# Storing the split gate weights in DRAM for a second pass of a state-space and gated-product kernel

## The chip, the cores and the metric

The kernel runs on one core of a Trainium2 chip. The core has a matrix engine (TensorE, PE in the profile; PEld is its weight load), a vector engine (VectorE, DVE), a scalar engine (ScalarE, ACT), GpSimd (POOL) and a sync engine (SyncE, SP) that only issues transfers; transfers run on 16 DMA engines. Each engine works through its own instructions in order and waits for others through semaphores. The metric is the device time of one execution in microseconds. A profile is one execution recorded by the hardware profiler.

## The reference

Everything is in fp32, for one sequence of 2048 tokens of width 640.

```python
mod = (_silu(c) @ w_mod).reshape(c.shape[0], 6, 1, -1)
sa, ca, ga, sb, cb, gb = (mod[:, 0], mod[:, 1], mod[:, 2], mod[:, 3], mod[:, 4], mod[:, 5])
h = _layernorm(x, axis=-1) * (1 + ca) + sa
x = x + ga * _A_ref(h, ...)          # a long convolution: kernel K from 192 complex modes a channel, by FFT
h = _layernorm(x, axis=-1) * (1 + cb) + sb
x = x + gb * _B_ref(h, ...)
...
def _B_ref(x, w_gate, w_up, w_down):     # w_gate, w_up: 640 x 1536, w_down: 1536 x 640
    g = jnp.einsum("bsd,df->bsf", x, w_gate)
    u = jnp.einsum("bsd,df->bsf", x, w_up)
    h = g * u
    return jnp.einsum("bsf,fd->bsd", h, w_down)
```

## The kernel before

There are two parts. The first, up to about 520 us, computes the modulation, the convolution kernel and the convolution. Its work is placed by a table of due times (`SCHED`): each unit (`u_d` is the last step of the convolution, `u_head` the start of the gated product) is advanced at written positions, and `SCHED["w"]` places the first loads and splits of gate weights among them. `u_d` loads two quarters of a transformed block (`TVa`, `TVb`, from `WD`) and the residual (`xsa`, `xsb`, from `A_u`) on the sync queue, multiplies on TensorE (L967), and adds the residual on DVE (L971 where the result stays in SBUF, L974 where it is stored). A row of matmuls without a use of its result (`warm`, L1149) runs in one gap.

The second part is the gated product. The 2048 tokens are worked in two halves (`for half in range(2)`), each of two token blocks of 512 columns. In a half, a loop over the 12 blocks `f` of 128 hidden columns computes gate and up products for both token blocks at once with a scheme that replaces eight products by seven with sums of weights and of tokens. After it come the down projections of the half's two token blocks (`down`, L1463), 12 steps each of 24 matmuls, and `fin`, which adds the residual and stores the output (L1475 and L1478).

TensorE multiplies in a reduced-precision form of fp32 (type `F32R`), and each product is made of three: high x high, high x low and low x high parts. So every weight and every activation is split by `hilo`: ACT copies it to the `F32R` type (the high part), DVE subtracts that from the value (the low part):

```python
def hilo(hi, lo, v):
    act(hi, v)
    V.tensor_tensor(lo, v, hi, op=OP.subtract)
```

The gate weights that the products `x_1` and `x_2` use come as pairs of blocks (`raw`, tile `wga`, 640 KB) and are split one block at a time by `split_g(i)` into `wsgh` and `wsgl`, four buffers each; the same buffers take the split down weights (`d_prep`). Block indices run to 24: block 12 + f of the second half has the same weights as block f of the first. `used` starts the next pair load after every second block. `raw_u` loads a gate block (`wgb`) and an up block (`wur`) again for the sums of weights; `sums_u` makes the sums on POOL (tile `tf`, L1036 to L1039) and `split_u` splits them (`wth`, `wtl`, `wsuh`, `wsul`). In a step of the loop `y_1`, `z_1`, `x_1`, `y_2`, `x_2`, `y_3`, `z_2` are groups of products, each in one of six PSUM banks; `y_2` has a sum on POOL (L1412), `y_3` a product on POOL (L1430). `split_g` is called four blocks ahead, between `y_2` and `sums_u`; the splits of blocks 12 to 14 are called in the last steps of the first half's last down projection, that of block 15 at the beginning of the second half. In the first half, `fold` also scales the down weights and stores them in DRAM (`wdg`).

The order of instructions on each engine and queue is that of the program from the second part on (a scheduler is off); in the first part it follows from the due times.

Of the kernel before, what the change touches and what calls it, by code (L numbers as in the profile page):

```python
# [10 lines left out]
F32 = mybir.dt.float32  # L11
# [7 lines left out]
P = 128  # L19
# [4 lines left out]
NB = D // P  # L24
NF = F // P
# [77 lines left out]
    k=(  # L103
        (189, 202),
        (208, 226),
        (356, 358),
        (499, 559),
        (422, 496),
        (634, 660),
        (663, 672),  # L110
        (698, 713),
# [37 lines left out]
    h=(2480, 2716, 2875, 2876, 2878, 2878, 2878, 2878),  # L149
    g=(  # L150
# [5 lines left out]
    ),  # L156
# [68 lines left out]
def tile_kernel(ctx: ExitStack, tc: tile.TileContext, I, out):  # L225
    nc = tc.nc
    V, S, G, PE, SY = nc.vector, nc.scalar, nc.gpsimd, nc.tensor, nc.sync

    def act(o, i, f=AF.Copy, **kw):
        return S.activation(o, i, f, **kw)  # L230
# [3 lines left out]
    dram1 = ctx.enter_context(tc.tile_pool(name="dram1", bufs=1, space=DRAM))  # L234
# [35 lines left out]
    def need(n, *k):  # L270

        assert done.get(k, 0) >= n, k
# [468 lines left out]
    def kg_pool(n, part):  # L741
        hf, s = divmod(n, 4)
        if part == 0:
            mk_ph(n)
            return
        mk_eq(n)
        mk_ep(n)
# [50 lines left out]
    def kg_ma(n):  # L798
        if n % 2 == 0:
            kg_of[n // 2] = ps_kg.tile([P, 8, 64], F32, name="kg")  # L800
        kg = kg_of[n // 2]
        PtA, QtA = OUT[n]["PA"], OUT[n]["QA"]
        for dl in range(4):
            dd = (n % 2) * 4 + dl
            for c in range(2):
                for j in range(4):
                    PE.matmul(kg[j * 32 : j * 32 + 32, dd, :], PtA[:, c, dl * 4 + j, :], QtA[:, c, dl * 4 + j, :],  # L807
                              start=dd == 0 and c == 0, stop=False, tile_position=(0, j * 32))
        if n % 2:
            need(0 if n < 8 else 4, "dsk")  # L810
            PE.matmul(kg[:, :, 0], ident, dskt[:, n - 1 : n + 1, :].rearrange("p t l -> p (t l)"), start=False, stop=False)

    def kg_mb(n):
        kg = kg_of[n // 2]
        PtB, QtB = OUT[n]["PB"], OUT[n]["QB"]
        for dl in range(4):
            dd = (n % 2) * 4 + dl
            for c in range(2):
                for j in range(4):
                    lo = (j % 2) * 64  # L820
                    r = dl * 2 + j // 2
                    PE.matmul(kg[j * 32 : j * 32 + 32, dd, :], PtB[lo : lo + 64, c, r, :], QtB[lo : lo + 64, c, r, :],  # L822
                              start=False, stop=dd == 7 and c == 1, tile_position=(lo, j * 32))

    def kg_out(n):

        Kt = ring(fp, [P, 8, 64], "Kt")
        act(Kt.rearrange("p d (b q) -> p d b q", q=4), kg_of[n // 2].rearrange("p d (q b) -> p d b q", q=4))
        KT[n // 2] = Kt
# [148 lines left out]
    WS, WU, WT, WR, UX, UE, AT = {}, {}, {}, {}, {}, {}, {}  # L978

    def mk(n, shape, dt_=F32, bufs=1):  # L980

        if n in FIRST:
            return FIRST.pop(n)
        return (wp if n in LEFT else gp).tile(shape, dt_, name=n, bufs=bufs)
# [4 lines left out]

    PAIRS = []  # L990
    for h in range(2):
        PAIRS += [("g", h * NF + 2 * p) for p in range(NF // 2)]
        PAIRS += [("d", 2 * h + T, 2 * p) for T in range(2) for p in range(NF // 2)]

    def raw():
# [15 lines left out]
    def used(f):  # L1011
        if f % 2 and PAIRS:
            raw()
# [11 lines left out]

    def split_g(i):
        WS[i] = mk("wsgh", [P, NB, P], F32R, 4), mk("wsgl", [P, NB, P], F32R, 4)
        hilo(*WS[i], WR.pop(("g", i)))
        if i > 3:
            used(i)  # L1030

# [175 lines left out]
    def at(ts, g, *a):  # L1207

        it = g(*a)
        for v in ts:  # L1210
            jobs.setdefault(v // 10, []).append((v, it))

    def once(f):
        def g(*a):
            f(*a)
            return
            yield
        return g
# [17 lines left out]
    def due(x):  # L1236
        for _, g in sorted(jobs.pop(x, []), key=lambda j: j[0]):
            next(g, None)
# [63 lines left out]
    for t in range(3 * NK + 24):  # L1302
        n, g = divmod(t, 3)
        k = n < NK
        if k:
            (kg_aq, kg_ap, kg_b)[g](n)
        due(2 * t)
        if k:
            for f in MUL.pop(0):
                f()  # L1310
        due(2 * t + 1)
        if g < 2 and n + 1 < NK:
            kg_pool(n + 1, g)
        if g == 0 and 0 < n <= NK:
            kg_mb(n - 1)
        if g == 1 and n % 2 == 0 and 0 < n <= NK:
            kg_out(n - 1)
        if g == 2 and k:
            kg_ma(n)
        if t == 3 * NK + 1:  # L1320
            kgp.close()
            PF.append(fft.enter_context(tc.tile_pool(name="ps_t", bufs=3, space=PSUM)))
            ps_g = ctx.enter_context(tc.tile_pool(name="ps_g", bufs=2, space=PSUM, side="right"))
            wp = ctx.enter_context(tc.tile_pool(name="wp", bufs=1, reuse_waits="tile"))
            wdg = dram1.tile([P, NF, D], F32, name="wdg")
            wv = [I[n].rearrange("(k p) f -> p k f", p=P) for n in ("B_w_gate", "B_w_up", "B_w_down")]

            def rows(tb):
                need(NB - 2, "d", tb)
                SY.dma_start(XB[tb][:, :, 0 : (NB - 2) * P], x2d[:, 4 * tb : 4 * tb + 4, 0 : (NB - 2) * P])  # L1330

            for j in range(2):
                XB[j] = mk(f"xb{j}", [P, 4, D])
                at(T0["wl"][j : j + 1], once(rows), j)
                at(T0["w"][j : j + 1], once(raw))
            for j in range(4):
                at(T0["w"][2 + j : 3 + j], once(split_g), j)
            at(T0["h"], u_head)
            at(T0["wm"][0:1], once(warm), 30)
            at(T0["wm"][1:2], once(warm), 4)  # L1340
# [191 lines left out]
    for half in range(2):  # L1532
# [37 lines left out]
        else:  # L1570
            for j in range(AHEAD):
                if LEAD <= j + 1 < AHEAD:
                    split_g(i0 + j + 1)
                x_1(i0 + j)
                x_2(i0 + j)
# [13 lines left out]
        for f in range(NF):  # L1589
            i = i0 + f  # L1590
            y_1(i)
            z_1(i)
            late = 0 < f <= NF - AHEAD
            if late:
                x_1(i + AHEAD - 1)
            if f + 1 < NF:
                split_u(i + 1, "a")
            y_2(i)
            if f + 1 < NF:
                split_u(i + 1, "bc")  # L1600
            if f + AHEAD < NF:
                split_g(i + AHEAD)
            if f + 2 < NF:
                sums_u(i + 2)
            if f + 3 < NF:
                raw_u(i + 3)
            if late:
                x_2(i + AHEAD - 1)
            y_3(i)
            z_2(i)  # L1610
            if half == 0:
                fold(f)
            if f >= NF - 2:
                d_prep(2 * half, f - NF + 2)
# [37 lines left out]
```

## Time and profile before

| | |
|---|---|
| time, median of 3 runs | 1004.66 us (1000.55 to 1005.87) |
| the profiled execution | 1001.29 us, span 999.2 us |
| busy: PE, DVE, ACT, POOL | 900.0, 762.8, 561.9, 564.3 us |
| moved by DMA | 153.16 MB, 153 GB/s on average |
| mean granted TensorE clock | 0.961 |

The span runs from the first to the last instruction; the execution's own time has 2.1 us more. Rows of groups give line, engine, operation, output <- inputs, shape and count, then busy time and mean ns. Rows of the timeline give start and length in us, engine, line, operation and, in brackets, the idle time before it with what ended it. SPq rows are issues on the sync queue, not the transfers themselves. Rows of DMA issues give count, KB of one and the median us from issue to landing. A chain row gives start, length and what the last-ending chain of work was doing.

### The profile page before, as it was taken

How to read it: one execution, taken by the hardware profiler on the slowest of the kernel's cores; microseconds unless marked ns; L12 is line 12 of the kernel's file. 1: busy time of each engine (PE TensorE's matmuls, PEld its weight loads, DVE VectorE, ACT ScalarE, POOL GpSimd, SP SyncE). 2: the span in 40 equal slices, each digit the busy share in tenths (PEclk: the TensorE clock that was granted, in tenths of full speed). 3: DMA queues.
4: the chain of work that ended last, by engine and by line, in shares of the span. 5: the costliest groups of instructions: out<-in, count | busy, mean ns of one | idle time of the engine just before them, and what ended most of it. 6: DMA issues, size and time to landing. Idle time of an engine off the chain costs nothing.

```text
span 999.2 us, 26832 instructions
## 1 busy us (share of the span) xinstructions
PE 900.0 (90%) x11192; PEld 727.2 (73%) x11192; DVE 762.8 (76%) x1399; ACT 561.9 (56%) x1048; POOL 564.3 (56%) x415
## 2 busy tenths in 40 slices
PE   4867898899789689998888999999999999999998
PEld 3565556675576467776555888879998888889998
DVE  8798569889979997975769788777576887768452
ACT  4869989987878979752354323235463422223331
POOL 5978899799789899930032667650112365542000
PEclk9877889999899899999999999999999999999999
DMA  8728754555256454577673442535635232212341
GB/s 265 254 50 301 227 176 135 194 163 167 68 163 202 129 161 120 164 248 214 210 210 123 153 150 87 184 132 159 209 134 202 88 105 80 79 53 59 100 159 53
DMA packets 147817, 153.16 MB, mean 153 GB/s; under 512 B 9200, under 2 KB 125424, under 8 KB 146288
## 3 DMA queue, kind: packets, MB, share of 16 engines
q1 hardware_dynamic: 145968, 148.43, 46.8%
q10 hardware_dynamic: 1728, 3.02, 0.8%
q8 instruction: 88, 1.44, 0.6%
q14 instruction: 33, 0.27, 0.1%
HBM read 110.45 MB, written 40.96 MB: 152 GB/s over the span
## 4 chain that ended last, share of the span: by engine, by line
PE 63%; DVE 16%; ACT 10%; issue 4%; DMA 4%; POOL 2%; SPq 1%; DVEq 0%; ACTq 0%; POOLq 0%
PE pa L1059 26%; PE pa L1463 16%; PE kg L807 2%; DMA xsb<-A_u 2%; PE kg L822 2%; PE psfc L889 2%; ACT L230 1%; PE psfb L889 1%; PE psfa L889 1%; PE psfc L946 1%; PE psfb L946 1%; PE psfa L946 1%; PE psfc L868 1%; ACT trb L230 1%; PE psfa L844 1%
## 5 line engine op out<-in xcount | busy, mean ns | idle before, releaser
L710 POOL TENSOR_TENSOR EQ<-LQ,RH 128x1536 f32<-128x1536 f32 x40 | 124.2, 3105 | 9.9 <-DVE QtB L767 9.7
L230 ACT ACTIVATE z<-pa 128x512 f32<-128x512 f32 x24 | 14.4, 598 | 175.7 <-POOL a L1430 112.1
L1024 DVE TENSOR_TENSOR wsgl<-wga,wsgh 128x640 fp32r<-128x640 f32 x72 | 70.0, 976 | 46.1 <-ACT wsgh L230 46.1
L1412 POOL TENSOR_TENSOR z<-z,s 128x512 f32<-128x512 f32 x24 | 32.1, 1337 | 126.5 <-DVE s L1411 72.0
L230 ACT ACTIVATE wsgh<-wga 128x640 fp32r<-128x640 f32 x72 | 52.5, 732 | 65.1 <-PE pa L1463 47.9
L1024 DVE TENSOR_TENSOR wtl<-tf,wth 128x256 fp32r<-128x256 f32 (+1 forms) x72 | 42.7, 594 | 48.3 <-ACT wth L230 48.3
L1463 PE MATMUL pa<-wsgh,sh 128*128 128x384 f32 (+1 forms) x304 | 69.4, 309 | 0.0
L1463 PE MATMUL pa<-wsgh,sl 128*128 128x384 f32 (+1 forms) x304 | 69.0, 308 | 0.0
L1463 PE MATMUL pa<-wsgl,sh 128*128 128x384 f32 (+1 forms) x304 | 69.0, 308 | 0.0
L710 POOL TENSOR_TENSOR Phb<-LH,DH 128x1536 int32<-128x1536 int32 x20 | 62.3, 3115 | 11.2 <-ACT tra L230 11.2
L710 POOL TENSOR_TENSOR EP<-LP,RH 128x768 f32<-128x768 f32 x40 | 66.1, 1651 | 0.0
L710 POOL TENSOR_TENSOR Pha<-LH,DH 128x1536 int32<-128x1536 int32 (+1 forms) x21 | 62.5, 2974 | 2.2 <-ACT trb L230 1.9
L1036 POOL TENSOR_TENSOR tf<-wur,wgb 128x256 f32<-128x256 f32 x23 | 17.8, 776 | 75.6 <-DVE wtl L1024 50.0
L822 PE MATMUL kg<-QtB,PtB 64*32 64x64 f32 x2560 | 48.7, 229 | 5.4 <-DVE QtB L766 5.3
L822 PEld LDWEIGHTS kg<-QtB,PtB 64*32 64x32 f32 x2560 | 41.6, 114 | 15.4 <-issue 6.5
L1463 PEld LDWEIGHTS pa<-wsgh,sl 128*128 128x128 f32 x304 | 46.4, 187 | 0.0
L1463 PEld LDWEIGHTS pa<-wsgl,sh 128*128 128x128 f32 x304 | 46.3, 187 | 0.0
L1059 PE MATMUL pa<-sh,wtl 128*128 128x512 f32 x144 | 45.0, 394 | 1.4 <-DVE wtl L1024 1.2
L1463 PEld LDWEIGHTS pa<-wsgh,sh 128*128 128x128 f32 x304 | 46.3, 187 | 0.0
L1059 PE MATMUL pa<-sh,wth 128*128 128x512 f32 x144 | 44.9, 393 | 0.5 <-ACT wth L230 0.5
L1059 PE MATMUL pa<-sl,wth 128*128 128x512 f32 x144 | 44.5, 390 | 0.0
L1430 POOL TENSOR_TENSOR a<-s,z 128x512 f32<-128x512 f32 x24 | 38.8, 1618 | 5.4 <-DVE s L1429 5.4
(604 smaller groups left out, 2925.2 us busy)
## 6 DMA issues: line engine op xcount, KB each, us to landing
wga<-wdg SPq DMA_DIRECT2D x24, 640.0 KB, 5.0
wga<-B_w_gate SPq DMA_DIRECT2D x12, 640.0 KB, 5.9
wgb<-B_w_gate SPq DMA_DIRECT2D x24, 320.0 KB, 3.4
wur<-B_w_up SPq DMA_DIRECT2D x24, 320.0 KB, 4.0
xb<-x2d SPq DMA_DIRECT2D x6, 1280.0 KB, 5.7
TVb<-WD SPq DMA_DIRECT2D x22, 256.0 KB, 3.6
t_tw<-w_mod SPq DMA_DIRECT2D x3, 1600.0 KB, 8.5
t_ti<-w_mod SPq DMA_DIRECT2D x3, 1600.0 KB, 7.9
```

Source lines behind the costliest of these rows:

```text
L230: return S.activation(o, i, f, **kw)
L710: G.tensor_tensor(o.rearrange("p x (h l) -> p x h l", l=8), lo.unsqueeze(2).to_broadcast([P, rows, nh, 8]), hi.rearrange("p h x -> p x h") ...
L807: PE.matmul(kg[j * 32 : j * 32 + 32, dd, :], PtA[:, c, dl * 4 + j, :], QtA[:, c, dl * 4 + j, :], start=dd == 0 and c == 0, stop=False, til ...
L822: PE.matmul(kg[j * 32 : j * 32 + 32, dd, :], PtB[lo : lo + 64, c, r, :], QtB[lo : lo + 64, c, r, :], start=False, stop=dd == 7 and c == 1, ...
L889: PE.matmul(r[c][par * 64 : par * 64 + 64, i, :], t_tw[:, k0 + k, c, :], src[:, k, :], start=True, stop=True, tile_position=(0, par * 64))
L946: PE.matmul(r[par][:, i], t_ti[lo : lo + 64, qd * 4 + i, c, :], x[lo : lo + 64, c, i, :], start=c == 0, stop=c == 1, tile_position=(lo, 0))
L1024: V.tensor_tensor(lo, v, hi, op=OP.subtract)
L1036: E.tensor_tensor(t[:, 0:2], u[:, 0:2], g[:, 0:2], op=OP.subtract)
L1059: PE.matmul(ps, w[a][:, k], x[b][:, l], start=n == 0 and m == 0, stop=n == 2 and m == len(ks) - 1)
L1412: G.tensor_tensor(ZT[i], ZT[i], S67[i], op=OP.add)
L1430: G.tensor_tensor(a_tile(NF + i % NF), c, ZT.pop(i), op=OP.mult)
L1463: PE.matmul(ACC[tb][t][c], x[:, ts], w[:, cs], start=st, stop=f == NF - 1 and n == 2 and (c == 0 or t % 2 == 1))
```

## The change

When the first half makes the high and the low part of a gate block, both are also stored to a DRAM tensor `wsd`, on the sync queue, 320 KB each. The second half no longer loads pairs of gate blocks for `x_1` and `x_2` and does not split them: for blocks 12 to 23 `split_g` issues two loads from `wsd` into `wsgh` and `wsgl` on GpSimd's queue. The DRAM tensor has the type fp32 and the tiles the type `F32R`, so the loads are casting transfers.

```diff
     PAIRS = []
     for h in range(2):
-        PAIRS += [("g", h * NF + 2 * p) for p in range(NF // 2)]
+        PAIRS += [("g", 2 * p) for p in range(NF // 2)] if h == 0 else []
         PAIRS += [("d", 2 * h + T, 2 * p) for T in range(2) for p in range(NF // 2)]
...
     def split_g(i):
         WS[i] = mk("wsgh", [P, NB, P], F32R, 4), mk("wsgl", [P, NB, P], F32R, 4)
+        if i >= NF:
+            for j in range(2):
+                G.dma_start(WS[i][j].rearrange("p k m -> p (k m)"), wsd[:, i - NF, j])
+            return
         hilo(*WS[i], WR.pop(("g", i)))
+        for j in range(2):
+            SY.dma_start(wsd[:, i, j], WS[i][j].rearrange("p k m -> p (k m)").bitcast(F32))
         if i > 3:
             used(i)
...
             wdg = dram1.tile([P, NF, D], F32, name="wdg")
+            wsd = dram1.tile([P, NF, 2, NB * P], F32, name="wsd")
```

## The prediction

> **What bounds the kernel now.** I read the busy time by stretch first, to see which stages have room at all, then the chain of work that ended last.
>
> ```profile
> 765.00:910.00 145.00, 145.00 (x634) 118.47 (x633) 106.18 (x157) 45.48 (x101) 66.83 (x63) 1.00 0.30 94
> 752.00:765.00 13.00, 11.45 (x71) 10.51 (x70) 10.73 (x16) 5.55 (x9) 5.57 (x4) 1.00 0.23 87
> 910.00:999.00 89.00, 84.98 (x578) 84.57 (x576) 41.61 (x65) 27.03 (x44) 1.64 (x2) 1.00 0.33 104
> ```
>
> The columns of the stretches are: stretch, length, busy us of PE, PEld, DVE, ACT, POOL, granted clock, share of the DMA engines, GB/s. In the second half's loop (765 to 910) PE is busy for all 145.00 us of 145.00, while DVE has 39 us and ACT 100 us idle. Only 1.55 us of PE time are missing in the turn between the halves (752 to 765). The chain that ended last says the same, and shows where PE is not the bound:
>
> ```profile
> 485.24 7.95 PE psg L1149 x34
> 494.97 3.20 DMA xsb<-A_u
> 498.98 4.86 DMA xsb<-A_u
> 503.96 0.69 DVE xsb L974
> 544.52 103.91 PE pa L1059 x451
> 761.34 149.04 PE pa L1059 x648
> 910.38 84.62 PE pa L1463 x576
> ```
>
> From 544.52 for 103.91 us and from 761.34 for 149.04 us the chain is one unbroken row of matmuls. Between 485 and 504, at the end of the convolution, it runs through loads of the sync queue. So the change works at three places: it relieves engines in the second half, where PE sets the time; it puts loads on GpSimd's queue there; and it puts stores into the sync queue where that queue sets the time.
>
> **What is removed.** Twelve high parts on ACT, twelve low parts on DVE, and six loads of a pair of gate blocks.
>
> ```profile
> L1024 DVE TENSOR_TENSOR wsgl<-wga,wsgh 128x640 fp32r<-128x640 f32 x72 | 70.0, 976 | 46.1 <-ACT wsgh L230 46.1
> L230 ACT ACTIVATE wsgh<-wga 128x640 fp32r<-128x640 f32 x72 | 52.5, 732 | 65.1 <-PE pa L1463 47.9
> 758.89 1.92 DVE L1024 TENSOR_TENSOR wsgl<-wga,wsgh 128x640 fp32r<-128x640 f32 x1
> 759.34 0.45 PE L1463 MATMUL pa<-wsgl,hh 128*128 128x384 f32 x2
> 760.74 0.55 DVE L1475 TENSOR_TENSOR xb<-pa,xb 128x384 f32<-128x384 f32 x1
> 761.34 0.73 PE L1059 MATMUL pa<-hh,wsgh 128*128 128x512 f32 x2 [1.55 <-DVE xb L1475]
> ```
>
> 12 x 0.976 = 11.7 us leave DVE and 12 x 0.732 = 8.8 us leave ACT, nearly all beside a PE that is full, so they buy nothing there. One of the twelve is on the path: the split of block 14 holds DVE from 758.89 to 760.8, the first sum of the finishing step (L1475) comes behind it, and the first matmul of the second half waits 1.55 us for that sum to free its PSUM bank. Without the split the sum can run while the last matmuls still do: **-1.5 us** (at least 1.0, because the sum still has to follow the matmuls of its own bank; at most 1.55, the whole gap). What is late next is then the matmul row itself.
>
> **What is added in the second half: 24 loads on GpSimd's queue.** In the loop the two loads of block i+4 stand behind POOL's sum L1412 of step i and ahead of the four sums of block i+2 and the product L1430. The products of the first stage (x_1) of step i+1 need them. One step, as it is now:
>
> ```profile
> 829.69 1.34 POOL L1412 TENSOR_TENSOR z<-z,s 128x512 f32<-128x512 f32 x1 [4.66 <-ACT wsgh L230]
> 842.09 1.34 POOL L1412 TENSOR_TENSOR z<-z,s 128x512 f32<-128x512 f32 x1 [4.81 <-ACT wsgh L230]
> 844.53 0.74 POOL L1036 TENSOR_TENSOR tf<-wur,wgb 128x256 f32<-128x256 f32 x1 [1.10 <-DVE wtl L1024]
> 845.47 0.51 SPq L1020 DMA_DIRECT2D wur<-B_w_up  x1
> 847.92 1.76 POOL L1430 TENSOR_TENSOR a<-s,z 128x512 f32<-128x512 f32 x1
> 849.89 0.62 PE L1059 MATMUL pa<-hh,wsgh 128*128 128x512 f32 x2
> 850.35 0.63 PE L1059 MATMUL pa<-hh,wsgl 128*128 128x512 f32 x2
> 850.15 0.60 ACT L230 ACTIVATE z<-pa 128x512 f32<-128x512 f32 x1 [8.10 <-PE pa L1059]
> wur<-B_w_up SPq DMA_DIRECT2D x24, 320.0 KB, 4.0
> wga<-B_w_gate SPq DMA_DIRECT2D x12, 640.0 KB, 5.9
> out<-xb SPq DMA_DIRECT2D x12, 320.0 KB, 3.1
> ```
>
> A step takes 842.09 - 829.69 = 12.40 us. POOL is free at 843.43; the matmul that reads the low part starts at 850.35 (the high part is read at 849.89). So issuing both loads and landing the second may take 850.35 - 843.43 = 6.9 us. Call T the time that POOL spends on one issue and L the time from issue to landing: the load is in time if 2T + L is at most 6.9. The trace shows no load issued by POOL and no casting one, so both are bounded. T: at least the 0.51 us of a sync-queue issue, at most the 1.76 us of POOL's longest operation here; I take 1.1, the middle. L: at least 3.1 us (a 320 KB transfer with rows of 2560 B), at most 5.9 us (the 640 KB gate load, as if the cast halved the rate). I take 4.5: the up-weight load of the same size takes 4.0 us, and that load and its neighbour start at about 845, at the same time as these two. 2 x 1.1 + 4.5 = 6.7 us: just in time. Between the ends, 4.1 and 9.4 us, the stall per step is 0 to 2.5 us. A stall repeats, because POOL's L1412 of the next step moves with PE: eight steps issue loads for a later step, so 0 to 20 us. I take 0.25 us x 8 = **+2 us**.
>
> The Trainium skill, page "DMA: Bandwidth & Descriptors", section "Anatomy of one DMA — SWDGE (gpsimd) path", gives 2.0 us + bytes/436e3 for such a transfer, 2.75 us for these 327,680 B. By it the two loads would be in time with room, and the sum would be 2 us lower; no row here shows a transfer from POOL.
>
> What is queued behind the loads on POOL: the sums L1036 to L1039 and L1430. They have waited 1.10 us at 844.53 for DVE, so 2T = 2.2 us makes them 1.1 us later. L1430 ends at 850.8 instead of 849.68; ACT's copy, which needs it and begins at 850.15 because of PE, slips by about 0.7 us, on an engine that idled 8.10 us before it. No PE time. A hit between DVE and POOL hides in the 39 us that DVE idles. At the turn, the loads for blocks 12 to 15 each wait on POOL for a down-projection step to free their buffer, and queued behind them are the sums of the second half's tokens, read later. Three pieces of PE work lie between that release and x_1: down steps of 24 matmuls (84.62/576 x 24 = 3.5 us) or blocks of 15 (12.40/54 x 15 = 3.4 us), so 10.4 us against 6.7. Cost zero, up to 3 us if POOL's first issues are much slower than the rest.
>
> **What is added in the first half: 24 stores of 320 KB on the sync queue.** Those of blocks 4 to 11 lie ahead of weight loads, here in one step:
>
> ```profile
> 592.37 0.37 SPq L1018 DMA_DIRECT2D wgb<-B_w_gate  x1
> 593.92 0.51 SPq L1002 DMA_DIRECT2D wga<-B_w_gate  x1
> 600.11 0.73 ACT L230 ACTIVATE wsgh<-wga 128x640 fp32r<-128x640 f32 x1
> ```
>
> A store of a low part waits for DVE's split, so wgb and wur go out some 2 us later; they are read a step of 12.40 us on, with about 4 us to land. The pair load wga now runs a step ahead of its splits; behind the stores it goes out at about 594 of the step before its use, lands 5.9 us later plus 2 us for the stores' data, at 602, and ACT's split of 600.11 slips by 2 us. ACT has 8 us of idle time behind it, and DVE and x_1 take the parts later still. Zero for PE, which is unbroken for 103.91 us; if that cover were gone, 2 us in every second step, 8 in all.
>
> The eight stores of blocks 0 to 3 are another matter. The changed program has four of them between the loads TVb/xsa and TVa/xsb, and four more between TVa/xsb and TVb/xsb:
>
> ```profile
> 488.07 0.91 SPq L959 DMA_DIRECT2D TVa<-WD  x2
> 489.64 0.99 SPq L959 DMA_DIRECT2D TVb<-WD  x2
> 494.97 0.37 SPq L961 DMA_DIRECT2D xsb<-A_u  x1
> 488.10 3.01 DVE L1024 TENSOR_TENSOR wsgl<-wga,wsgh 128x640 fp32r<-128x640 f32 x4
> 494.25 0.69 DVE L971 TENSOR_TENSOR xb<-psfc,xsb 128x512 f32<-128x512 f32 x1 [2.53 <-PE psfc L967]
> 498.26 0.69 DVE L971 TENSOR_TENSOR xb<-psfa,xsb 128x512 f32<-128x512 f32 x1
> 488.00:490.00 2.00, 2.00 (x10) 1.65 (x10) 2.00 (x4) 0.35 (x1) 0.00 (x0) 1.00 0.23 69
> 490.00:492.00 2.00, 2.00 (x11) 1.65 (x10) 1.72 (x3) 0.00 (x0) 0.00 (x0) 1.00 1.11 315
> 494.00:496.00 2.00, 1.79 (x12) 0.31 (x8) 1.71 (x7) 0.00 (x0) 0.00 (x0) 1.00 0.01 2
> TVb<-WD SPq DMA_DIRECT2D x22, 256.0 KB, 3.6
> ```
>
> The first store goes early. The second waits for the first of DVE's four splits, 488.10 + 3.01/4 = 488.9; the third and fourth follow at about 0.5 us each, the fourth behind the second split. So TVa is issued at 490.4, not 488.07, and TVb, behind four more stores, at about 494, not 489.64. Their data count too. Three stores (0.98 MB), TVa (0.52) and xsb (0.26) make 1.77 MB; the engines, at 315 GB/s when full and with some 1.5 us from issue to full flow, need until 488.9 + 1.5 + 5.6 = 496. L971 then comes at about 497 instead of 494.25. Four more stores (1.31 MB) and TVb (0.52) take 5.8 us more, to 501.8, and with the matmuls of 1 to 1.5 us the second L971 stands at about 503 instead of 498.26: +5. The next xsb load waits for it as it does now and takes its 4.86 us, and L974, which heads the in-order DVE queue at 503.96, moves along. Everything up to 544 follows from that queue. **+5 us**. The lower end: if the stores' data did not delay the loads, TVa 2.3 us and TVb 4.4 us later on the queue would eat slack (matmuls of L1149 fill PE until 493.19; all data are in by 494.00, 4.3 us ahead of the second L971) and cost +1. The upper end, with the stores at half that rate, is +8. A gain is excluded: the order of the queue is fixed.
>
> **Sum.** -1.5 + 2 + 5 = +5.5 us. The profiled execution took 1001.29 us (span 999.2 and 2.1 around it); that makes 1006.8 there. The median of the runs shown is 3.4 us above that execution, so the forecast against the median 1004.66 is 1010.2.
>
> **Rivals.** *The casting loads land late* (POOL issues slowly, or the cast halves the rate): 2T + L of 9.4 us, 2.5 us in each of eight steps: +20 - 1.5 + 5 = +23.5, 1028. Decided where 2T + L passes 6.9 us; for it speak POOL's long operations (1.76 us) and a DVE that is busy 106 of 145 us and may get in POOL's way; against it, the 3.1 us store row. The Trainium skill, page "SBUF — State Buffer", section "SBUF: two separate sides", warns that DVE in a two-port mode keeps GpSimd from writing descriptors, which would put the loads into this rival; the same page's section "Who interferes with whom" exempts the two-input subtraction, which is most of what DVE runs here, and no run yet shows it.
>
> *The stores are absorbed*, so that it is not slower: the transfers of the tail drain fast enough that the second L971 comes by 499.3. Then the end of the convolution costs +1, the loads are in time, and the turn gains 1.5: -0.5, 1004.2. Decided by whether TVb lands before 498; for it speak engines idle at 494 to 496 (2 GB/s), against it that 2.6 MB of stores need 8.3 us at 315 GB/s in a window that has 2 us free.
>
> *Relief counts for more* than the one gap: impossible from the rows by more than a little, as PE has 1.55 us idle in the turn, none in the loop, and 4.02 us at the very end, where the output leaves: at most -5.
>
> **How the numbers follow.** Forecast case (+2 to +9) 0.52, late loads (+9 to +25) 0.25, absorbed (-3 to +2) 0.17, relief or something not seen 0.06. 0.5% is 5.0 us, about what a measurement can tell from no change. Of the forecast case two thirds lie above that (its upper ends are farther off than its lower ones): 0.35 + 0.25 = 0.60 slower. Faster by 0.5% gets the last case's 0.06. The rest, 0.34, is no change. The range leaves out the end of the late loads and the last case: 1003 to 1028.
>
> **What would show it.** Right: the stores' issues at 489 to 494 ahead of TVb, the second L971 at about 503, the first matmul at the turn without a gap, x_1 in the loop waiting for a DMA by no more than 0.5 us, no wsgh or wsgl of ACT and DVE between 749 and 900 but those of the down weights. Wrong: a loop that takes more than 150 us, x_1 waiting 1 us or more each step (the late loads), or a second L971 before 500 (absorbed).

## The result, and the profile after

| | before | changed |
|---|---|---|
| median of 20 runs | 1002.23 us (998.09 to 1005.87) | 1005.91 us (1002.95 to 1011.38) |
| ratio | | 1.0044, 95% interval 1.0027 to 1.0060 |
| the profiled execution | 1001.29 us, span 999.2 | 1010.92 us, span 1009.1 |

The change makes the kernel slower by 0.44%: the means of the 20 runs are 4.4 us apart, the medians in the table 3.7 us. The forecast was +5.5 us; its 1010.2 us was counted from the median 1004.66 us of the runs shown at that time, and from 1002.23 us it is 1007.7. The two profiled executions differ by more, 9.9 us of span, so the first thing to settle is where. The chain of work of the changed kernel:

```profile
495.10 3.85 DMA TVa<-WD
500.31 4.95 DMA TVb<-WD
505.40 3.42 PE psfa L967 x8
553.80 103.91 PE pa L1065 x451
769.03 21.01 PE pa L1065 x90
793.50 3.92 DMA wsgl<-wsd
797.47 122.11 PE pa L1065 x532
919.57 84.63 PE pa L1470 x576
```

Against the rows of before, the first unbroken row of matmuls begins 553.80 - 544.52 = 9.28 us later, the second half 769.03 - 761.34 = 7.69 us later, its down projections 919.57 - 910.38 = 9.19 us later. But the changed kernel is late before it has run anything that the change touches. The loads TVb of the sync queue, just ahead of the first new store, come at 484.36 in place of 479.61:

```profile
479.61 0.91 SPq L959 DMA_DIRECT2D TVb<-WD  x2
```

```profile
484.36 0.91 SPq L959 DMA_DIRECT2D TVb<-WD  x2
485.92 0.45 SPq L1034 DMA_DIRECT2D wsd<-wsgh  x1
493.69 0.33 SPq L1034 DMA_DIRECT2D wsd<-wsgl  x1
494.11 0.38 SPq L1034 DMA_DIRECT2D wsd<-wsgh  x1
494.59 0.41 SPq L1034 DMA_DIRECT2D wsd<-wsgl  x1
495.10 1.56 SPq L959 DMA_DIRECT2D TVa<-WD  x2
496.72 0.68 SPq L961 DMA_DIRECT2D xsb<-A_u  x1
...
498.99 1.23 SPq L1034 DMA_DIRECT2D wsd<-wsgl  x1
500.31 2.24 SPq L959 DMA_DIRECT2D TVb<-WD  x2
```

Those 4.75 us come from the stage before. The stretch from 250 to 300 us of both kernels, before and then changed, has a granted clock (the third number from the right) of 0.90 and of 0.80, and TensorE runs 944 matmuls in it and 862:

```profile
250.00:300.00 50.00, 41.40 (x944) 32.66 (x936) 43.60 (x80) 41.69 (x82) 39.55 (x26) 0.90 0.37 113
```

```profile
250.00:300.00 50.00, 42.61 (x862) 33.58 (x856) 41.25 (x77) 39.55 (x78) 36.90 (x25) 0.80 0.36 109
```

Why the clock differs is not shown. But all nine kernels of this study run the same instructions up to those TVb loads and issue them between 476.71 and 484.36, the earliest two at 476.71 without the new DRAM tensor and at 477.27 with it, so this is the spread of that stage and not the change. From here on, kernels are compared by three stretches: the **tail** (from those TVb loads to the first matmul of the unbroken row), the **turn** (from there to the first matmul of the second half) and the **loop** (from there to its down projections). Each is a difference of two rows of one profile.

| kernel | TVb issue | tail | turn | loop | ratio to before |
|---|---|---|---|---|---|
| before | 479.61 | 64.9 | 216.8 | 149.0 | 1 |
| changed | 484.36 | 69.4 | 215.2 | 150.5 | 1.0044 (1.0027 to 1.0060) |
| stores only | 481.30 | 69.7 | 216.9 | 149.1 | 1.0054 (1.0033 to 1.0075) |
| stores only, a fifth of the tail's data | 477.27 | 66.0 | 216.9 | 149.0 | 1.0023 (1.0007 to 1.0038) |
| deferred stores | 481.67 | 65.5 | 215.0 | 150.0 | 1.0000 (0.9984 to 1.0017) |
| deferred stores, early loads | 478.19 | 64.8 | 214.9 | 148.8 | 0.9977 (0.9958 to 0.9996) |
| tail's stores on ACT's queue | 481.66 | 76.2 | 214.8 | 150.0 | 1.0126 (1.0100 to 1.0152) |
| two blocks only | 478.65 | 64.1 | 215.3 | 148.8 | 0.9976 (0.9960 to 0.9993) |
| one split moved, no DRAM | 476.71 | 64.0 | 215.3 | 148.8 | 0.9985 (0.9966 to 1.0004) |

For the change: +4.5 in the tail, -1.6 in the turn, +1.5 in the loop, +4.4 us in sum. That it is the measured 4.4 us to the tenth is chance: each stretch is read from one profile, and the kernels without stores in the tail have tails of 64.0 to 65.5 us, so a difference of 1 us in that column says little.

The tail, read on DVE and TensorE of the changed kernel, as the same lines were read before:

```profile
492.85 3.01 DVE L1024 TENSOR_TENSOR wsgl<-wga,wsgh 128x640 fp32r<-128x640 f32 x4
501.38 0.69 DVE L971 TENSOR_TENSOR xb<-psfc,xsb 128x512 f32<-128x512 f32 x1 [4.91 <-DMA xsb<-A_u]
505.40 3.42 PE L967 MATMUL psfa<-TVb,ct 64*32 64x512 f32 x8 [4.47 <-DMA TVb<-WD]
508.86 0.69 DVE L971 TENSOR_TENSOR xb<-psfa,xsb 128x512 f32<-128x512 f32 x1 [3.60 <-PE psfa L967]
512.94 0.68 DVE L974 TENSOR_TENSOR xsb<-psfa,xsb 128x512 f32<-128x512 f32 x1
501.00:504.00 3.00, 0.00 (x0) 0.00 (x0) 2.37 (x10) 0.15 (x1) 0.00 (x0) 0.86 1.03 377
504.00:506.00 2.00, 0.60 (x2) 0.21 (x4) 1.00 (x6) 0.76 (x3) 0.57 (x2) 0.50 1.07 310
```

The sync queue waits for DVE's splits at 492.85 to put the low parts out; the loads TVa and TVb go out behind the stores; the DMA engines are full (share 1.03 and 1.07) while TensorE waits 4.47 us for TVb. When it comes, the granted clock has dropped to 0.50 and the eight matmuls take 3.42 us instead of the 1.74 us of before. The kernel before has the same dip, but there it meets the next group, that of TVa, which the changed kernel runs at full clock. Here are three rows of before and then that group in the changed kernel:

```profile
494.06 1.74 PE L967 MATMUL psfa<-TVb,ct 64*32 64x512 f32 x8
500.98 2.61 PE L967 MATMUL psfa<-TVa,ct 64*32 64x512 f32 x8 [0.56 <-DMA TVa<-WD]
502.00:504.00 2.00, 2.00 (x10) 0.48 (x3) 0.63 (x2) 1.37 (x3) 1.05 (x3) 0.50 1.13 334
```

```profile
510.36 1.42 PE L967 MATMUL psfa<-TVa,ct 64*32 64x512 f32 x8
```

Both groups together take 3.42 + 1.42 = 4.84 us in place of 1.74 + 2.61 = 4.35, so the dip cost 0.5 us more of TensorE's time than before and not 1.7. A dip to 0.50 at this place is in all nine traces.

The turn and the loop of the changed kernel:

```profile
768.58 0.46 PE L1470 MATMUL pa<-wsgl,hh 128*128 128x384 f32 x2
768.87 0.62 PE L1065 MATMUL pa<-hh,wsgh 128*128 128x512 f32 x2
796.21 0.73 PE L1065 MATMUL pa<-hh,wsgh 128*128 128x512 f32 x2 [0.70 <-DMA wsgh<-wsd]
797.47 0.74 PE L1065 MATMUL pa<-hh,wsgl 128*128 128x512 f32 x2 [0.53 <-DMA wsgl<-wsd]
```

The second half begins right behind the last down matmul, where 1.55 us had stood. In the kernel before, the split that held DVE there (758.89) took 1.92 us, where the one at 750.23 took 0.83. A sum on POOL ran beside it until 760.13, and the split ended 0.68 us after that sum:

```profile
758.38 1.75 POOL L1389 TENSOR_TENSOR s<-a,a 128x512 f32<-128x512 f32 x1
```

The split at 754.02 took 1.69 us and ended 0.69 us behind a POOL sum in the same way. So about 1 us of the gap (an estimate: 1.92 - 0.83) may come from meeting POOL's sum and not from the split's own work. No run here parts the two: those that remove or move this split take it out of both.

In the loop of the changed kernel TensorE waits in one place, 0.70 and 0.53 us for the two parts of the first block loaded in it; after that the matmuls are unbroken for 122.11 us. On POOL a later step looks like this:

```profile
838.89 1.34 POOL L1419 TENSOR_TENSOR z<-z,s 128x512 f32<-128x512 f32 x1 [5.23 <-DVE s L1418]
840.17 0.59 POOL L1030 DMA_DIRECT2D wsgh<-wsd  x1
840.76 0.54 POOL L1030 DMA_DIRECT2D wsgl<-wsd  x1
841.34 0.74 POOL L1042 TENSOR_TENSOR tf<-wur,wgb 128x256 f32<-128x256 f32 x1
```

From the sum L1419 to the first sum of weights it is 841.34 - 838.89 = 2.45 us; it was 844.53 - 842.09 = 2.44 us before. The two issues fit into the time that POOL had waited for DVE.

### The profile page after: what moved, and what is told of

Same layout as the page of the kernel before. It is cut to its first block, busy times and chain, and to the rows that moved or that the text cites. A ratio compares the mean times of both kernels' runs of the same rounds, so it can differ in the third digit from the quotient of the medians.

```text
span 1009.1 us, 26878 instructions
## 1 busy us (share of the span) xinstructions
PE 909.5 (90%) x11192; PEld 734.6 (73%) x11192; DVE 751.1 (74%) x1387; ACT 554.9 (55%) x1036; POOL 572.8 (57%) x439
## 4 chain that ended last, share of the span: by engine, by line
PE 63%; DVE 15%; ACT 11%; DMA 4%; issue 4%; POOL 2%; SPq 0%; DVEq 0%; ACTq 0%; POOLq 0%
PE pa L1065 25%; PE pa L1470 16%; PE kg L807 2%; PE psfc L889 2%; PE kg L822 2%; PE psfb L889 2%; ACT L230 2%; PE psfa L889 1%; PE psfc L868 1%; PE psfc L946 1%; ACT trb L230 1%; PE psfb L946 1%; PE psfa L946 1%; DMA xsb<-A_u 1%; PE psfb L844 1%
## 5 line engine op out<-in xcount | busy, mean ns | idle before, releaser
L1419 POOL TENSOR_TENSOR z<-z,s 128x512 f32<-128x512 f32 x24 | 32.0, 1335 | 127.6 <-DVE s L1418 124.6
L1024 DVE TENSOR_TENSOR wsgl<-wga,wsgh 128x640 fp32r<-128x640 f32 x60 | 53.7, 900 | 43.3 <-ACT wsgh L230 43.3
L230 ACT ACTIVATE wsgh<-wga 128x640 fp32r<-128x640 f32 x60 | 43.8, 733 | 65.0 <-PE pa L1470 47.0
```

What stands on the lines that cost most here:

```text
L1419: G.tensor_tensor(ZT[i], ZT[i], S67[i], op=OP.add)
```

## The experiments

**Stores without loads.** The second half is as before the change; the 24 stores remain.

```diff
-        PAIRS += [("g", 2 * p) for p in range(NF // 2)] if h == 0 else []
+        PAIRS += [("g", h * NF + 2 * p) for p in range(NF // 2)]
...
-        if i >= NF:
-            for j in range(2):
-                G.dma_start(WS[i][j].rearrange("p k m -> p (k m)"), wsd[:, i - NF, j])
-            return
...
-        for j in range(2):
+        for j in range(2 if i < NF else 0):
             SY.dma_start(wsd[:, i, j], WS[i][j].rearrange("p k m -> p (k m)").bitcast(F32))
```

Expected:

> All 24 stores as in the change, but the second half loads and splits its gate weights as before the change. Three stretches are read: the tail of the convolution (from the issue of the TVb loads at 479.61 in the kernel before, 484.36 in the changed one, to the first matmul of the unbroken row: 64.9 us before, 69.4 us changed), the turn (from there to the first matmul of the second half: 216.8 and 215.2 us), the loop (to the first matmul of its down projections: 149.0 and 150.5 us). Theory (the eight stores at the tail cost, the loads nearly nothing): tail 69.4, turn 216.8, loop 149.0; in all +4.5 us, ratio 1.0045. Rival 1 (the casting loads cost, the stores are absorbed): all three as before, ratio 1.000. Rival 2 (the 4.75 us by which the changed kernel is late already at the TVb loads comes from the change): late there by some 5 us again.

Measured: tail 69.7, turn 216.9, loop 149.1, ratio 1.0054. The stores alone cost 4.8 us of the tail, and the gap at the turn is back (the first matmul of the second half again waits 1.57 us for L1478, which is L1475 of before). The first rival falls. So does the second: this kernel reaches the TVb loads at 481.30, 3 us ahead of the changed one.

**A fifth of the data.** As that kernel, with fewer bytes in the tail's stores.

```diff
+            if i < 4:
+                SY.dma_start(wsd[:, i, j, :P], WS[i][j][:, 0].bitcast(F32))
+            else:
+                SY.dma_start(wsd[:, i, j], WS[i][j].rearrange("p k m -> p (k m)").bitcast(F32))
```

> As the stores-only kernel, but the eight stores at the tail carry only the first of five 128-column pieces of each part (64 KB in place of 320), with the same number of issues and the same waits for ACT and DVE; the rest of those parts is not stored. It tells the wait in the queue from the data. Theory (data of 2.6 MB ahead of the loads): the tail falls from 69.4 to 66 to 67 us (+1 to +2, from loads issued 2.3 to 4.4 us later). Rival (the sync queue's waits and issues alone): the tail stays at 69 us.

Measured: tail 66.0 us. The loads go out nearly as late as with all the data, but they land sooner: TensorE waits 2.67 us for TVb, where it waited 4.49 us in the kernel with all 24 stores in full:

```profile
491.58 1.04 SPq L959 DMA_DIRECT2D TVb<-WD  x2
495.66 2.62 PE L967 MATMUL psfa<-TVb,ct 64*32 64x512 f32 x8 [2.67 <-DMA TVb<-WD]
498.32 0.69 DVE L971 TENSOR_TENSOR xb<-psfa,xsb 128x512 f32<-128x512 f32 x1 [1.26 <-PE psfa L967]
```

TVb goes out 491.58 - 477.27 = 14.3 us after the first TVb loads, where it was 10.0 before and 16.0 with all the data. So 69.7 - 66.0 = 3.7 us of the 4.8 are the bytes (2.1 MB fewer), and 1.1 us the waits, the issues and the fifth that is left, as far as a scatter of about 1 us lets one say.

**Deferred stores.** The stores of blocks 0 to 3 stand behind the convolution's last transfers; their buffers are not needed again until the first step of the loop.

```diff
-        for j in range(2):
-            SY.dma_start(wsd[:, i, j], WS[i][j].rearrange("p k m -> p (k m)").bitcast(F32))
+        if i < 4:
+            LATE_ST.append((i, WS[i]))
+        else:
+            store_g(i, WS[i])
...
             raw()
+            while LATE_ST:
+                store_g(*LATE_ST.pop(0))
             raw_u(2)
```

> The changed kernel, with the eight stores of blocks 0 to 3 issued after the convolution's last loads and stores, behind the third pair load of the first half. Theory: tail back to 64.9 us, turn 215.2, loop 150.5; in all -0.1 us against before, ratio 1.000 (0.998 to 1.002). Rival 1 (the casting loads cost): 1.004 as the change. Rival 2 (the stores only move their cost to the start of the first half): tail 67 to 69 us.

Measured: tail 65.5, turn 215.0, loop 150.0, ratio 1.0000. The eight stores are now issued from 522.41 to 529.6 on the queue:

```profile
522.41 0.33 SPq L1030 DMA_DIRECT2D wsd<-wsgh  x1
...
529.16 0.44 SPq L1030 DMA_DIRECT2D wsd<-wsgl  x1
```

They delay nothing there: from the row of matmuls at 523.54 to the unbroken row at 547.15 it is 23.61 us, and from 520.91 to 544.52 it was the same 23.61 us before. The loss of the change is gone with their place. What is left is the gain at the turn and the one wait in the loop.

**Early loads.** That kernel, and in the second half `split_g` is called at the beginning of a step.

```diff
             i = i0 + f
+            if f + AHEAD < NF and half:
+                split_g(i + AHEAD)
             y_1(i)
...
-            if f + AHEAD < NF:
+            if f + AHEAD < NF and half == 0:
                 split_g(i + AHEAD)
```

> The kernel with deferred stores, and in the second half the two loads of a block stand at the beginning of the step, ahead of POOL's sum L1412, in place of behind it. Theory (the 1.5 us of the loop are one wait, in the second step, for a load issued late in the first step): loop 149.0 to 149.2 us, turn 215.2, tail 64.9; -1.6 us against before, ratio 0.998. Rival (the loads are slow wherever they stand, or disturb DVE): loop 150.5 us or more, ratio 1.000.

Measured: loop 148.8, ratio 0.9977, faster than both the kernel before and the changed one. The loads stand in a gap that POOL has between the product of one step and the sum of the next, and no step waits for them:

```profile
831.39 1.81 POOL L1445 TENSOR_TENSOR a<-s,z 128x512 f32<-128x512 f32 x1
833.13 0.59 POOL L1036 DMA_DIRECT2D wsgh<-wsd  x1
833.72 0.54 POOL L1036 DMA_DIRECT2D wsgl<-wsd  x1
838.43 1.33 POOL L1427 TENSOR_TENSOR z<-z,s 128x512 f32<-128x512 f32 x1 [4.18 <-DVE s L1426]
757.93 148.77 PE pa L1073 x648
```

**The tail's stores on ACT's queue.** A different queue for the same bytes, to part the order in one queue from the traffic.

```diff
-            SY.dma_start(wsd[:, i, j], WS[i][j].rearrange("p k m -> p (k m)").bitcast(F32))
+            (S if i < 4 else SY).dma_start(wsd[:, i, j], WS[i][j].rearrange("p k m -> p (k m)").bitcast(F32))
```

> The changed kernel, with the eight stores of blocks 0 to 3 issued on the scalar engine's queue in place of the sync queue: the same data at the same place, but no load stands behind a store in the sync queue. Theory (after the run with a fifth of the data: 3.7 of the 4.8 us are the data): tail between 67 and 69 us, turn 215.0, loop 150.0 to 150.5; against before +2 to +4 us. Rival (what costs is being ahead of the loads in one queue, and transfers of another queue hardly slow them): tail 65 to 66 us, as with deferred stores.

Measured: tail 76.2 us, ratio 1.0126. Neither theory said so. The issue of the first low part waits for DVE, and it now waits on the engine that has to copy the convolution's results out of PSUM:

```profile
480.17 0.33 ACTq L1034 DMA_DIRECT2D wsd<-wsgh  x1
490.99 0.33 ACTq L1034 DMA_DIRECT2D wsd<-wsgl  x1
491.37 0.74 ACT L230 ACTIVATE wsgh<-wga 128x640 fp32r<-128x640 f32 x1 [11.23 <-DVE wsgl L1024]
493.36 0.60 ACT L230 ACTIVATE Wa<-psfa 128x512 f32<-128x512 f32 x1 [1.26 <-DVE wsgl L1024]
```

ACT stands for 11.23 us, and 76.2 - 64.9 = 11.3 us are lost. The question it was to answer, what the bytes cost without the order in one queue, it does not answer: the wait hides it.

**Two blocks only.** Of the twelve blocks, only 14 and 15 come from DRAM; blocks 2 and 3 are stored, deferred.

```diff
-        PAIRS += [("g", 2 * p) for p in range(NF // 2)] if h == 0 else []
+        PAIRS += [("g", h * NF + 2 * p) for p in range(NF // 2) if h == 0 or p != 1]
...
-        if i >= NF:
+        if i in (14, 15):
```

> Only the parts of blocks 2 and 3 are stored (four stores, deferred), and only blocks 14 and 15 are loaded by POOL in the second half; the other ten are loaded and split as before. Theory (of the twelve splits taken from DVE and ACT, that of block 14 alone lies on the path): the whole gain at the turn, 215.0 us in place of 216.8; tail 64.9, loop 149.0; -1.8 us against before, ratio 0.998. Rival (the gain comes from several of the splits, or from the loads of pairs that are left out): turn 216 us or more, ratio 0.999 to 1.000.

Measured: turn 215.3, loop 148.8, ratio 0.9976. Ten of the twelve splits are back on DVE and ACT, the turn is within 0.1 us of the changed kernel's 215.2, and TensorE has no gap in it between the halves. Removing those ten bought nothing that shows.

**One split moved.** The kernel before, without any of the change; only the call for block 14 stands behind the finishing sums.

```diff
-                    elif h2:
+                    elif h2 and n < NF + 2:
                         split_g(n)
...
             for j in range(AHEAD):
+                if j == 0:
+                    split_g(i0 + 2)
                 if LEAD <= j + 1 < AHEAD:
```

> The kernel before, with nothing stored or loaded through DRAM; only the split of block 14 is called after the finishing sums of the first half's last token block instead of ahead of them. Theory (the gain at the turn is the order of that one split on DVE, not the work saved): turn 215.0 to 215.5 us in place of 216.8, tail 64.9, loop 149.0; -1.5 us, ratio 0.9985. Rival (DVE is short of time at the turn, so the split only stalls the products of block 14 a few us later): turn 215.3 us and loop 150 to 151 us, ratio 1.000.

Measured: turn 215.3, loop 148.8, ratio 0.9985. The profile shows the split now behind the eight sums, with no wait in TensorE for block 14:

```profile
755.05 0.55 DVE L1475 TENSOR_TENSOR xb<-pa,xb 128x384 f32<-128x384 f32 x1
...
757.90 0.41 DVE L1478 TENSOR_TENSOR xb<-pa,xb 128x256 f32<-128x256 f32 x1
759.44 0.81 DVE L1024 TENSOR_TENSOR wsgl<-wga,wsgh 128x640 fp32r<-128x640 f32 x1
755.95 148.77 PE pa L1059 x648
```

The ratio's interval just includes 1, so the time alone does not prove 1.5 us. The turn does: 215.3 us, where the three kernels with this split ahead of the sums have 216.8 or 216.9 and the five others 214.8 to 215.3. Whatever the change gained came from the place of one subtraction, and can be had without storing anything.

## Why the prediction was right, point by point

*The removed work.* Forecast: -1.5 us at the turn, nothing elsewhere. Measured -1.6, and -1.5 again with only two blocks, or with one split moved. Right, and for the reason given, the place of one split ahead of the finishing sums; that the 1.92 us of this split may be more than half a wait for POOL's sum was not seen.

*The stores of blocks 0 to 3.* Forecast +5, measured +4.5. The steps, taken 4.75 us off the changed kernel's rows: TVa out at 490.35 (forecast 490.4), TVb at 495.56 (about 494), the first L971 at 496.63 (497), the second at 504.11 (503). The data of TVb were not late: they landed at 500.51 (500.31 + 4.95 - 4.75), where 501.8 had been said. The second L971 was later than said because the eight matmuls, for which the sum had 1 to 1.5 us, took 3.42 us at half the clock. The next load gave part of it back: the forecast let it take its 4.86 us again, but it took 2.8 us (issued at 509.58), and L974, which had waited 1.37 us for its DMA before, found its data there and came 4.2 us late in place of 5.85. So the path was right, the matmuls were sized too short and the last load too long, and that the sum came within 0.5 us is in part luck. Bounds of +1 for queue order alone and the rest for the data were about what the run with a fifth of the data showed (1.1 and 3.7 us).

*The stores of blocks 4 to 11.* Forecast zero, and the unbroken row of the first half is 103.91 us in both kernels.

*The loads.* Forecast +2 us, measured +1.5, but not in the way forecast: here two errors offset each other, and that the sizes agree is luck. T was 0.54 to 0.60 us in the steps and 0.77 us for the very first issue, not 1.1; L was 3.7 us in the median (3.2 to 6.5), not 4.5. 2T + L is then 4.8 us against a window of 6.9. (L in the rows counts from the start of the issue, so T + L, 4.3 us, is the time to compare.) Seven of the eight steps do not wait at all, where 0.25 us each was said. The eighth is the first step, whose window I had taken to be like the others. It is not: that step has no `x_2`, nine matmuls fewer (2.1 us), and POOL's sum comes later in it. The kernel before shows this already:

```profile
784.25 1.32 POOL L1412 TENSOR_TENSOR z<-z,s 128x512 f32<-128x512 f32 x1 [24.12 <-DVE s L1411]
788.35 0.63 PE L1059 MATMUL pa<-hh,wsgl 128*128 128x512 f32 x2
```

There POOL is free at 785.57, and TensorE reads the low part at 788.35, 2.8 us later. In the changed kernel, from POOL's free moment at 792.93 to the point where TensorE could have read the low part (795.12 + 2 matmul groups of 0.23 and 0.46, so 795.8) it is 2.9 us, and the low part landed 4.5 us after that moment (793.50 + 3.92 = 797.42). The turn's four blocks came in time, as said.

By the formula of the Trainium skill, page "DMA: Bandwidth & Descriptors", section "Anatomy of one DMA — SWDGE (gpsimd) path", a transfer of this size takes an estimated 2.75 us. The runs show 3.2 at the least and 3.7 in the median, beside other transfers, so here the measured numbers count; by the formula the steady steps do not wait either, and they do not. The warning of the Trainium skill, page "SBUF — State Buffer", section "SBUF: two separate sides", that DVE in a two-port mode keeps GpSimd from writing descriptors, was not put to the test, as DVE ran only operations of two inputs in the loop. Beside its subtractions an issue took 0.54 to 0.60 us, which agrees with the exemption in the Trainium skill, same page, section "Who interferes with whom".

At the turn one sum of DVE that began during an issue (at 762.63) took 2.47 us in place of 0.69 and ended 0.55 us behind POOL's next sum. What held it is not shown; TensorE did not wait for it.

*The rivals.* Late loads: out, the loop took 150.5 us and not 169. Absorbed stores: out, the second L971 came 5.85 us late. Relief: only the one gap was there to win.

*The signs.* Two of the signs named were not kept. x_1 waited 0.70 and 0.53 us, where no more than 0.5 was to be seen, and the loop took 150.5 us, where more than 150 was to show it wrong; that limit did not fit the forecast itself, whose +2 us asks for 151. And 0.44% is just under the 0.5% that was to part slower from no change; the forecast gave 0.60 to slower and 0.34 to no change, and the interval of 0.27 to 0.60% leaves open which it is.

## What to carry to other kernels

A transfer that nobody waits for can still cost, here 4.5 us, through what stands behind it in its queue: put stores of intermediate results where the queue has nothing urgent behind them, and never an issue that waits for a slow producer on an engine that has to compute next. Work taken off an engine beside a full TensorE is worth only the pieces that end a wait; find those in the turn between stages, and try first whether reordering one instruction gets the same. A window measured in a steady step does not hold for the first step of the loop, so read that one by itself.

## What the runs showed of the hardware that was not expected

An issue of a 320 KB casting load cost POOL 0.54 to 0.60 us, hardly more than the 0.51 us of a sync-queue issue, and the first one 0.77 us. The granted clock fell to 0.50 for a short while at the end of the convolution in every kernel of this study, and a late load changed which matmuls met it: in the changed kernel the group of TVb took 3.42 us in place of 1.74, and the next one 1.42 in place of 2.61. And a DVE subtraction that ran beside a POOL sum took 1.92 us in place of 0.83.
